# Batch 0's second softmax with the tokens on the partitions: products by chunks of 128 tokens, the way back by TensorE

## The chip, the cores and the metric

The kernel runs on one core of one Trainium2 chip. The metric is the device time of one execution in microseconds (us); smaller is better. Engines are called by the names of the profile: PE (TensorE's matmuls), PEld (its weight loads), DVE (VectorE), ACT (ScalarE), POOL (GpSimd), SP (SyncE, which issues the DMAs here).

## The reference

For each of 8 batches and 8 heads 32 packed rows `p` attend over 576 keys (first softmax), and 576 queries `q` attend over the 32 packed rows (second softmax). The result, read as 4608 tokens by 512, goes through a gated feed-forward layer. All data are fp32.

```python
def sm_attn(qq, kk, vv):
    s = scale * np.matmul(qq, kk.transpose(0, 1, 3, 2))
    s = s - np.max(s, axis=-1, keepdims=True)
    a = np.exp(s)
    a = a / (np.sum(a, axis=-1, keepdims=True) + 1e-09)
    return np.matmul(a, vv)
p_packed = sm_attn(p, k, v)
out = sm_attn(q, p_packed, p_packed)
...
return (x @ w_a) * (x @ w_b) @ w_out
```

## The kernel before

The second attention's value product is folded into the weights: with `pp` the packed rows, `g = pp @ w` for each tile of 128 columns of `w_a` and `w_b` (`g_tiles`, L382), and the layer's first product is then the softmax weights times `g`. The weights of the second softmax, called a2, lie with 4 heads x 32 packed rows on the 128 partitions and the 576 tokens along the row; there are two such groups, e = 0 and 1. a2 and `g` are both split into a high part (`a2_hi`, `ghi`, rounded to the fp32r type) and the rest (`a2_lo`, `glo`), and each product is made of three: hi x hi, hi x lo, lo x hi.

Batch 0 goes first and its chain of steps has nothing to run beside it but the conversion of the weights: load q, k, v, p; turn them by TensorE (`turn_first`, L141, one step `k0`..`k4`, `q0`..`q4` each); first softmax (`stage1`, L265, steps `S0`, `S1`, `r0`, `r1`); `turned` (L254, step `P0`) puts the packed rows into `ppT`; second softmax (`stage2`, L335, steps `s0` for e = 0 and `s1` for e = 1); the first `g` (`next_g`, L594, step `g`); then the loop over 12 column tiles ft (`mm1`, L419), each with two halves of six units, a unit being one pair of `ghi`/`glo` with `a2_hi`/`a2_lo` over 2 x 288 tokens, and then the layer's second product (`mm2_part`). The rest of the kernel (batches 1 to 7) follows without a break.

The second softmax of batch 0, for each e, as the lines stand: L341 makes the scores in PSUM, 8 products with 32 columns of `ppT` as weights and 288 tokens moving, so the packed rows lie on the partitions; L346 (DVE) turns each 32x32 block, which brings the tokens to the partitions in blocks and the 32 scores of one token into a row; L350 (DVE) takes the maximum over these 32; L353 subtracts it (POOL for e = 0, DVE for e = 1); L355 (ACT) is exp; L359 to L361 (DVE) sum and reciprocal; L362 multiplies (POOL for e = 0, DVE for e = 1); L366 (DVE) turns the blocks back; L372 (ACT) writes `a2_hi`; L374 writes `a2_lo` (DVE for e = 0, POOL for e = 1, by way of `lo_part`, L93).

The order of every engine is written out by hand: `START` (L528) is the list of steps up to the first `mm1`, and `PLAN_0` (L539) is what is put between the halves of the loop over ft. Each engine runs its instructions in the order in which these lists emit them. Beside the steps above the lists hold: `A`, `B`, `C`, the three steps that convert one piece of weights (L201 on ACT; L209 on ACT or L206 on DVE or POOL, by the digit of `WAYS`: 0, 1, 2; L212 on DVE), a piece being 128 x 512 words, with four pieces needed for one `g_tiles`; `D`, a split of `w_out`; `L..`, loads; and `X`, `Y`, `Z` with a number, so many products of zeros (L592) that keep TensorE running while it has nothing else. `X` takes a bank of the pool of two single banks, `Z` a pair of banks of the pool of two pairs called m, `Y` the one pair called s. The scores of e = 0 lie in the pair s, those of e = 1 in a pair m. `FIRST` is the order of the first loads, `TURN` picks DVE or ACT for the copies of `turn_first`, `SUBS`, `MULS`, `LOWS`, `HLO`, `WLO` pick the engine of single steps.

## Time and profile before

| what | value |
|---|---|
| median of 3 runs | 708.05 us (707.85 to 708.61) |
| profiled execution, its own time | 707.41 us |
| its span | 705.6 us |
| PE busy | 699.4 us (99%), 5654 matmuls |
| PEld busy | 582.8 us (83%) |
| DVE, ACT, POOL busy | 455.9 us (65%), 356.9 us (51%), 417.1 us (59%) |
| chain that ended last, by engine | PE 91%, DVE 4%, ACT, DMA, SP and issue 1% each |

The page gives the busy time of each engine and the chain of work that ended last, followed back from the end. A matmul's row lasts longer than the time after which the next can start, so a busy PE says little about small gaps: these are read from the starts of neighbouring rows. The first `mm1` starts 31.16 us after the span's start; what comes ahead of it is the stretch that the change rewrites.

### The profile page before, as it was taken

Reading aid. Unit: us, or ns where it says so; the run is one execution under the profiler, and the core shown is the slowest. Engines: PE = TensorE matmul, PEld = TensorE weight load, DVE = VectorE, ACT = ScalarE, POOL = GpSimd, SP = SyncE. Lnnn points to the kernel's source line nnn. Section 1 sums busy time; section 2 is a strip of 40 time slices with the busy share of each in tenths; the row PEclk is TensorE's granted clock in tenths of the full one; section 3 lists DMA queues with packets and bytes.
Section 4 is the critical chain, followed back from the end, with each engine's and each line's share of the span. In section 5 each row is a group of like instructions: output and inputs, shape, how many; then the busy total and the mean of one; then the engine's idle time right before and its main releaser. Section 6 shows DMA issues by size and latency. Waiting matters only on the chain.

```text
span 705.6 us, 14386 instructions
## 1 busy us (share of the span) xinstructions
PE 699.4 (99%) x5654; PEld 582.8 (83%) x5654; DVE 455.9 (65%) x833; ACT 356.9 (51%) x719; POOL 417.1 (59%) x321
## 2 busy tenths in 40 slices
PE   9999999999999999999999999999999999999998
PEld 7888878898788888878888788888888878888886
DVE  4997765467365679566775678765785667754332
ACT  3778724554244555535554455554545446544520
POOL 1596741337254777646863589566775578856520
PEclk9999999999999999999999999999999999999999
DMA  9999986753254736356434664556145323133002
GB/s 316 380 229 297 282 233 136 252 106 93 69 141 161 170 89 172 115 139 168 119 95 124 173 161 95 131 165 173 63 123 154 106 91 119 60 124 117 1 1 75
DMA packets 179460, 102.65 MB, mean 145 GB/s; under 512 B 145728, under 2 KB 161344, under 8 KB 174016
## 3 DMA queue, kind: packets, MB, share of 16 engines
q1 hardware_dynamic: 179392, 101.73, 50.7%
q8 instruction: 44, 0.72, 0.4%
q14 instruction: 24, 0.20, 0.1%
HBM read 85.98 MB, written 15.73 MB: 144 GB/s over the span
## 4 chain that ended last, share of the span: by engine, by line
PE 91%; DVE 4%; issue 1%; DMA 1%; ACT 1%; SPq 1%; DVEq 0%
PE x L754 36%; PE m L796 28%; PE m L414 11%; PE m L440 5%; PE x L810 4%; PE s L326 2%; PE s L341 1%; PE x L396 1%; PE s L280 1%; DMA qn<-in_q_dram 1%; PE s L316 1%; DVE a_lo L93 1%; DVE part L764 0%; DVE d L878 0%; DVE w_ab L212 0%
## 5 line engine op out<-in xcount | busy, mean ns | idle before, releaser
L754 PE MATMUL x<-wo,h_hi 128*128 128x512 f32 (+1 forms) x776 | 249.4, 391 | 0.0
L93 POOL TENSOR_TENSOR h_lo<-asb,h_hi 128x576 fp32r<-128x576 f32 x95 | 139.0, 1465 | 76.0 <-ACT h_hi L841 42.8
L754 PEld LDWEIGHTS x<-wo,h_hi 128*128 128x128 f32 x776 | 140.8, 188 | 22.1 <-ACT part L762 0.8
L754 PE MATMUL x<-wo,h_lo 128*128 128x512 f32 (+1 forms) x388 | 152.2, 392 | 0.0
L93 POOL TENSOR_TENSOR G_lo<-gs,G_hi 128x640 fp32r<-128x640 f32 x72 | 113.1, 1577 | 29.6 <-ACT G_hi L831 29.4
L754 PEld LDWEIGHTS x<-wo,h_lo 128*128 128x128 f32 x388 | 72.9, 188 | 11.7
L93 POOL TENSOR_TENSOR A_lo<-gs,A_hi 128x256 fp32r<-128x256 f32 x36 | 27.2, 755 | 89.3 <-ACT A_hi L819 89.3
L878 DVE TENSOR_TENSOR d<-m,d 128x576 f32<-128x576 f32 (+1 forms) x73 | 54.1, 741 | 34.7 <-ACT d L874 33.9
L891 DVE TENSOR_TENSOR asb<-m,d 128x288 f32<-128x288 f32 x72 | 32.5, 451 | 63.2 <-ACT c L887 59.9
L887 ACT COPY c<-m 128x288 f32<-128x288 f32 x72 | 28.8, 400 | 82.5 <-PE m L796 82.5
L764 DVE TENSOR_TENSOR part<-x,part 128x512 f32<-128x512 f32 (+1 forms) x65 | 44.1, 678 | 38.8 <-PE x L754 38.8
L796 PE MATMUL m<-tx_hi,G_hi 128*128 128x288 f32 x216 | 63.8, 296 | 0.0
L796 PE MATMUL m<-tx_hi,G_lo 128*128 128x288 f32 x216 | 63.6, 295 | 0.0
L796 PE MATMUL m<-tx_lo,G_hi 128*128 128x288 f32 x216 | 63.2, 293 | 0.0
L816 ACT COPY gs<-x 128x512 f32<-128x512 f32 x35 | 20.6, 588 | 82.2 <-PE x L810 80.6
L831 ACT CAST G_hi<-gs 128x640 fp32r<-128x640 f32 x72 | 52.2, 729 | 15.7 <-POOL gs L825 15.1
L874 ACT COPY d<-m 128x576 f32<-128x576 f32 (+1 forms) x73 | 46.7, 640 | 19.2 <-PE m L796 18.8
L841 ACT CAST h_hi<-asb 128x576 fp32r<-128x576 f32 x72 | 49.0, 680 | 11.5 <-DVE asb L905 11.5
L796 PEld LDWEIGHTS m<-a_hi,G_hi 128*128 128x128 f32 x144 | 27.0, 187 | 31.9 <-issue 17.4
L825 POOL TENSOR_TENSOR gs<-gs 128x512 f32<-128x512 f32 x36 | 46.7, 1297 | 3.2 <-DVE gs L822 2.9
L796 PE MATMUL m<-a_hi,G_hi 128*128 128x288 f32 x144 | 46.6, 324 | 0.0
L904 DVE TENSOR_TENSOR m<-m,c 128x288 f32<-128x288 f32 x72 | 33.3, 463 | 17.0 <-PE m L796 15.3
(189 smaller groups left out, 1568.9 us busy)
## 6 DMA issues: line engine op xcount, KB each, us to landing
wr<-w_kept SPq DMA_DIRECT2D x36, 1024.0 KB, 5.1
nat<-in_k_dram SPq DMA_DIRECT2D x56, 144.0 KB, 4.7
nat<-in_q_dram SPq DMA_DIRECT2D x56, 144.0 KB, 5.3
vt<-in_v_dram SPq DMA_DIRECT2D x28, 256.0 KB, 3.9
out_dram<-part SPq DMA_DIRECT2D x27, 256.0 KB, 2.1
raw<-in_moe_w_a_dram SPq DMA_DIRECT2D x12, 512.0 KB, 8.7
raw<-in_moe_w_b_dram SPq DMA_DIRECT2D x12, 512.0 KB, 8.7
raw<-in_moe_w_out_dram SPq DMA_DIRECT2D x12, 512.0 KB, 6.9
```

The costliest lines, as they stand in the source:

```text
L93: return eng.tensor_tensor(out=dst, in0=src, in1=hi.bitcast(F32), op=ALU.subtract)
L414: nc.tensor.matmul(out=ps[:, half, 0:HS], lhsT=gt[:, kt, ft % 4, cols], rhs=at[:, kt, HS * half:HS * half + HS], start=(n == 0 and kt == 0 ...
L440: nc.tensor.matmul(out=o[:, cols], lhsT=ht[:, c0:c0 + P], rhs=wt[:, cols], start=(ft == 0 and n == 0), stop=(ft == NFT - 1 and n == 2))
L754: nc.tensor.matmul(out=o[:, cols], lhsT=ht[:, c0:c0 + P], rhs=wt[:, cols], start=(ft == fts[0] and n == 0), stop=end)
L764: nc.vector.tensor_tensor(out=parts[i][:, cols], in0=o[:, cols], in1=parts[i][:, cols], op=ALU.add)
L796: nc.tensor.matmul(out=bank[:, n % 2, 0:HS], lhsT=g, rhs=t, start=(first and i == 0), stop=(i == 2), skip_group_check=True)
L825: nc.gpsimd.tensor_tensor(out=gs[:, 2:4].rearrange("p a u f -> p a (u f)"), in0=gs[:, 0:2].rearrange("p a u f -> p a (u f)"), in1=s2.unsqu ...
L831: nc.scalar.copy(out=G_hi[:, n % 3], in_=gs[:, 1:6, n % 2])
L841: nc.scalar.copy(out=view(h_hi[ft]), in_=src)
L874: nc.scalar.copy(out=d[:, both], in_=X[:, both, 0:HS])
L878: nc.vector.tensor_tensor(out=d[:, both], in0=V[:, both, 0:HS], in1=d[:, both], op=ALU.add)
L904: nc.vector.tensor_tensor(out=v, in0=v, in1=c2, op=ALU.add)
```

## The change

For batch 0 alone `stage2` makes the scores with the tokens on the partitions. For each e there are 24 products in place of 8: for chunks c = 0 and 1 the weights are 128 tokens of `q` (64 rows x 128 columns) and the 32 columns of `ppT` move; for c = 2 the weights are the last 32 tokens. L346's turn goes; the maximum reads PSUM; the difference reads PSUM and is on DVE for both e. Exp, sum, reciprocal and product stay. L366's turn back goes: for each e TensorE turns four blocks of 128 x 128 and makes eight products of 32 x 32 with the identity, into a pair of banks; `a2_hi` (ACT) and `a2_lo` (DVE for both e) read that pair. The first `g`'s two low parts become steps of their own. The first `mm1` runs its twelve units in the order of `MIX` (ten units, the copy of the first half, two units). `START`, `PLAN_0`, `FIRST` and the strings of engines are new: the zero products between the second softmax's scores and `g` are 25 in place of 50, `k0 p0 k1 q0 v0 v1 q1` is the order of the first loads, and the same conversions lie at other places. `PLAN_0` is cut here to its first line.

```diff
@@ -336,21 +336,34 @@
 
         TU = 2 * XH
         x = bank_pair(b > 0 or e == 0)
-        for r in range(R):
-            for u in range(2):
-                nc.tensor.matmul(
-                    out=x[J * r:J * r + J, u, 0:HS], lhsT=ppT[64 * u:64 * u + 64, 1 if u ^ e else 2 * (b % 2), r, :],
-                    rhs=xT_cols(b, "q", u, 2 * r + e), start=True, stop=True)
+        qk = lambda u, r: ppT[64 * u:64 * u + 64, 1 if u ^ e else 2 * (b % 2), r, :]
+        for c, r, u in [(c, r, u) for c in (range(3) if b == 0 else (0,)) for r in range(R) for u in range(2)]:
+            xT = xT_cols(b, "q", u, 2 * r + e)
+            if b:
+                nc.tensor.matmul(out=x[J * r:J * r + J, u, 0:HS], lhsT=qk(u, r), rhs=xT, start=True, stop=True)
+            elif c < 2:
+                at = P * c + J * r
+                nc.tensor.matmul(out=x[:, u, at:at + J], lhsT=xT[:, P * c:P * c + P], rhs=qk(u, r), start=True, stop=True)
+            else:
+                nc.tensor.matmul(out=x[J * r:J * r + J, u, 2 * P:HS], lhsT=xT[:, 2 * P:HS], rhs=qk(u, r), start=True, stop=True)
         yield
         s2 = work(b, f"s2_{e}", [P, TU, J], "t1")
-        nc.vector.transpose(out=s2.rearrange("p (u x) j -> p u (x j)", u=2), in_=x[:, :, 0:HS])
+        if b:
+            nc.vector.transpose(out=s2.rearrange("p (u x) j -> p u (x j)", u=2), in_=x[:, :, 0:HS])
         if b > NB:
             yield
         mx = sm.tile([P, TU], F32, name="mx")
-        nc.vector.tensor_reduce(out=mx, in_=s2, axis=AX, op=ALU.max)
+        four = lambda t: t.rearrange("p (u x) j -> p u x j", u=2)
+        raw2 = s2 if b else x[:, :, 0:HS].rearrange("p u (x j) -> p u x j", j=J)
+        nc.vector.tensor_reduce(
+            out=mx if b else mx.rearrange("p (u x) -> p u x", u=2), in_=raw2, axis=AX, op=ALU.max)
         yield
         on = lambda flags: nc.vector if b < 2 and flags[2 * b + e] == "1" else nc.gpsimd
-        on(SUBS).tensor_tensor(out=s2, in0=s2, in1=mx.unsqueeze(2).broadcast_to([P, TU, J]), op=ALU.subtract)
+        peak = mx.unsqueeze(2).broadcast_to([P, TU, J])
+        if b:
+            on(SUBS).tensor_tensor(out=s2, in0=s2, in1=peak, op=ALU.subtract)
+        else:
+            nc.vector.tensor_tensor(out=four(s2), in0=raw2, in1=four(peak), op=ALU.subtract)
         yield
         nc.scalar.activation(out=s2, in_=s2, func=AF.Exp, scale=scale)
         yield
@@ -361,6 +374,22 @@
         nc.vector.reciprocal(out=sum2, in_=sum2)
         on(MULS).tensor_tensor(out=s2, in0=s2, in1=sum2.unsqueeze(2).broadcast_to([P, TU, J]), op=ALU.mult)
         yield
+        if b == 0:
+            y = bank_pair(e == 1)
+            for u in range(2):
+                at = s2[:, XH * u:XH * u + XH, :].rearrange("p x j -> p (x j)")
+                for c in range(2):
+                    nc.tensor.transpose(y[:, u, P * c:P * c + P], at[:, P * c:P * c + P], ident)
+                for r in range(R):
+                    z = slice(J * r, J * r + J)
+                    nc.tensor.matmul(out=y[z, u, 2 * P:HS], lhsT=at[z, 2 * P:HS], rhs=ident[z, z], start=True, stop=True)
+            a2f = y[:, :, 0:HS].rearrange("p u (x l) -> p u x l", l=TL)
+            hi, lo = (t[:, e, :].rearrange("p (x u l) -> p u x l", u=2, l=TL) for t in (a2_hi, a2_lo))
+            nc.scalar.copy(out=hi, in_=a2f)
+            yield
+            lo_part(lo, a2f, hi)
+            yield
+            return
         halves = b >= NB
         a2f = work(b, f"a2f_{e}", [P, 2, XH, TL], "t1" if halves and e else "t2")
         nc.vector.transpose(out=a2f.rearrange("p u x l -> p (u x l)"), in_=s2.rearrange("p x j -> p (x j)"))
@@ -397,10 +426,15 @@
                         out=gps[e][J * r:J * r + J, 0:2 * P * n], lhsT=ppT[rows, 2 * (b % 2), r, :],
                         rhs=w if n == 2 else w[:, fts[0] % 2], start=True, stop=True)
             parts = [(x, slice(0, E))] if x is not None else [(gps[e][:, 0:2 * P * n], e) for e in range(E)]
+            lows = []
             for part, e in parts:
                 hi, lo = (t[:, e, i] if n == 1 else t[:, e, i:i + 2].rearrange("p u c -> p (u c)") for t in (ghi, glo))
                 nc.scalar.copy(out=hi, in_=part)
-                lo_part(lo, part, hi)
+                if s and b == 0:
+                    lows.append((lo, part, hi))
+                else:
+                    lo_part(lo, part, hi)
+        return lows
 
 
     def mm1_half(i, ft, ps=None, kts=range(E)):
@@ -416,16 +450,33 @@
                     start=(n == 0 and kt == 0), stop=(n == len(steps) - 1 and kt == E - 1))
         return ps
 
+    def first_units(ps, order, n0, n1):
+
+        halves = [i for i, _ in order]
+        for n in range(n0, n1):
+            i, unit = order[n]
+            kt, what = divmod(unit, 3)
+            gt, at = ((ghi, a2_hi), (ghi, a2_lo), (glo, a2_hi))[what]
+            for half in range(2):
+                nc.tensor.matmul(
+                    out=ps[i][:, half, 0:HS], lhsT=gt[:, kt, 0, P * i:P * i + P], rhs=at[:, kt, HS * half:HS * half + HS],
+                    start=i not in halves[:n], stop=i not in halves[n + 1:])
+
     def mm1(b, ft, between):
         asb = sm.tile([P, 2, HS], F32, name="asb")
         if b == 0 and ft == 0:
-            pa, pb = (mm1_half(i, ft, kts=(0,)) for i in range(2))
-            mm1_half(0, ft, pa, (1,))
+            order = [divmod(int(x, 16), 6) for x in MIX]
+            last = max(n for n, (i, _) in enumerate(order) if i == 0)
+            pa, pb = both = bank_pair(), bank_pair()
+            first_units(both, order, 0, last + 1)
+            nc.scalar.copy(out=asb, in_=pa[:, :, 0:HS])
+            between()
+            first_units(both, order, last + 1, 12)
         else:
-            pa, pb = mm1_half(0, ft), None
-        nc.scalar.copy(out=asb, in_=pa[:, :, 0:HS])
-        between()
-        pb = mm1_half(1, ft, pb, (1,) if pb is not None else range(E))
+            pa = mm1_half(0, ft)
+            nc.scalar.copy(out=asb, in_=pa[:, :, 0:HS])
+            between()
+            pb = mm1_half(1, ft)
         nc.vector.tensor_tensor(out=asb, in0=pb[:, :, 0:HS], in1=asb, op=ALU.mult)
         c0 = 64 * (b % 2)
         hh = h_hi[ft][:, c0:c0 + S]
@@ -524,23 +575,24 @@
 
     st = {}
 
-    FIRST = ("k0 k1 p0 q0 v0 q1 v1 w1 w1 w1 w1 w1 w1 w1 w1 w1 w1 w1")
-    START = ("Y7 k1 X4 k0 T0 k2 k3 k4 q1 B S0 r0 r1 S1 q0 r1 r0 q2 r0 r1 q4 r0 r1 q3 A P0 A X3 Lp2 A s0 s1 s0 "
-             "s1 C Z8 s1 X3 s0 B A B Z9 C B X7 A B C C X5 X15 C s0 A s1 B s0 s1 A B Lk2 B B A s0 B s1 s1 C s0 "
-             "s1 g A")
-    WAYS = ("200000020222122211202100021202110111")
-    TURN = ("1000100010")
-    SUBS, MULS, LOWS = "0101", "0100", "01"
-    HLO, WLO = "000000001000", "000011000011"
+    FIRST = ("k0 p0 k1 q0 v0 v1 q1 w1 w1 w1 w1 w1 w1 w1 w1 w1 w1 w1")
+    START = ("Y8 k1 k0 k2 T0 k3 k4 q1 S0 r0 r1 S1 q0 B r1 r0 r0 r1 r0 q2 A r1 q3 q4 P0 A s1 Lp2 s0 s1 A C s0 B "
+             "C B C X8 s1 s0 B A B C A Y12 A C Z1 s0 X2 B B s0 B s1 Z2 Lk2 B A s0 A s1 B s1 s0 s1 s1 C A g g g "
+             "A")
+    WAYS = ("220000010222122211100100021212120112")
+    TURN = ("0010100010")
+    SUBS, MULS, LOWS = "1010", "0111", "01"
+    HLO, WLO = "000000001101", "000011000011"
+    MIX = "019428a7356b"
 
     PLAN = (" |  |  | S0 | r0 | r0 |  | r0 |  | r0 Lv1 ; S1 | r1 | r1 q0 Lk2 | r1 | r1 | q1 Lk3 Lv2 P0 |  ; s0 | s0 s0 | s0 T2 | "
             "s0 Lp4 | s0 s1 | s1 s1 | s1 | s1 | s1 | t0 t1 t2 t3 u0 | k2 |  | k3 Lq2")
     PLAN = dict(enumerate(PLAN.split("|")))
-    PLAN_0 = ("Lk1 A A B C B C B A C | C B C | A A B | B C A A C A C | | B Lp2 C Lv0 B | | | C k0 T0 B | A A C "
...
+    PLAN_0 = ("A B C B Lk1 A C B C B C | B C | A A A A | B C A Lp2 B C | C | B A C | | | C k0 T0 A A B | C Lv0 "
...
     PLAN_0 = dict(enumerate(PLAN_0.split("|")))
 
     pieces = [(c, n) for c in range(NC) for n in range(4)] + [(NC, f) for f in range(NFT)]
@@ -593,7 +645,9 @@
 
     def next_g(b):
 
-        g_tiles(b, *(((0, 1), (2,)) if b else ((0, 1),)), s=True)
+        for lo, part, hi in g_tiles(b, *(((0, 1), (2,)) if b else ((0, 1),)), s=True):
+            yield
+            lo_part(lo, part, hi)
         yield
 
     ET = mybir.EngineType
```

## Rows read from the trace of the kernel before

**Rows 1.** The table of windows, two of its stretches: start and end, length, then for PE, PEld, DVE, ACT, POOL the busy time with the number of instructions, PE's granted clock, the DMA engines' share, GB/s.

```profile
35.00:45.00 10.00, 10.00 (x91) 8.16 (x76) 8.56 (x12) 8.70 (x17) 9.51 (x7) 1.00 0.92 202
225.00:706.00 481.00, 477.12 (x3590) 396.78 (x3588) 308.96 (x583) 235.69 (x488) 308.32 (x241) 1.00 0.42 117
```

**Rows 2.** The chain of work that ended last, pieces between 17 and 35 us: start, length, engine, tile and line.

```profile
17.26 0.73 PE s L341 x16
...
18.01 0.79 DVE s L346
...
22.24 2.49 DVE w_ab L212 x4
...
27.58 0.99 DVE s L362
28.57 0.70 DVE a2f L366
...
29.29 1.33 ACT a_hi L372 x2
30.62 0.49 ACT ghi L402
...
31.16 3.72 PE m L414 x24
```

**Rows 3.** The same chain between 71 and 78 us.

```profile
71.42 0.59 ACT ghi L402
72.01 0.55 ACT asb L426
...
72.60 5.07 PE m L414 x36
```

**Rows 4.** The timeline of SP's queue: start, length, line and what is loaded (the second part of q, then the second group of v).

```profile
5.15 0.45 SPq L138 DMA_DIRECT2D qn<-in_q_dram  x1
...
6.15 0.39 SPq L170 DMA_DIRECT2D vt<-in_v_dram  x1
```

**Rows 5.** The DMA view of the same two loads: size and us from issue to landing.

```profile
qn<-in_q_dram SPq DMA_DIRECT2D x1, 640.0 KB, 6.4
...
vt<-in_v_dram SPq DMA_DIRECT2D x1, 512.0 KB, 7.2
```

**Rows 6.** The timeline of PE: start, length to the last end, line, tiles, rows x columns of the weights, what moves, and how many instructions (an fp32 product is two).

```profile
1.05 3.36 PE L592 MATMUL s<-zero 128*128 128x128 f32 x14 [1.05 <-DVE zero L77]
...
12.19 0.66 PE L316 MATMUL x<-ident,a 128*128 128x128 f32 x4
...
13.64 0.38 PE L152 MATMUL x<-ident,qn 128*128 128x128 f32 x2
13.95 1.78 PE L326 MATMUL x<-vt,a1T 128*32 128x64 f32 x80
...
17.19 0.72 PE L341 MATMUL s<-qT,ppT 64*32 64x288 f32 x16
17.70 0.70 PE L341 MATMUL m<-qT,ppT 64*32 64x288 f32 x16
...
20.88 2.17 PE L592 MATMUL m<-zero 128*128 128x128 f32 x18
...
29.02 1.21 PE L396 MATMUL x<-w_ab,ppT 64*32 64x512 f32 x16
31.16 0.54 PE L414 MATMUL m<-a_hi,ghi 128*128 128x288 f32 x2 [0.93 <-ACT ghi L402]
```

**Rows 7.** Single lines' instructions between 14 and 45 us (L592, L341) and 31 and 35 us (L414): shortest, median and longest duration in ns, first and last start, form.

```profile
L592 PE MATMUL m<-zero x34: 275/275/377, 18.3 to 22.8; 128*128 128x128 f32 x34
...
L341 PE MATMUL s<-qT,ppT x16: 402/413/427, 17.2 to 17.5; 64*32 64x288 f32 x16
...
L414 PE MATMUL m<-a_hi,ghi x8: 294/297/402, 31.2 to 34.1; 128*128 128x288 f32 x8
```

**Rows 8.** The timeline of PEld, the weight loads of L341's first group.

```profile
17.19 0.19 PEld L341 LDWEIGHTS s<-qT,ppT 64*32 64x32 f32 x16
```

**Rows 9.** The timeline of DVE between 20 and 30 us.

```profile
20.30 0.76 DVE L350 TENSOR_REDUCE mx<-s 128x18 f32<-128x576 f32 x1
20.97 0.69 DVE L212 SCALAR_TENSOR_TENSOR w_ab<-raw 128x512 uint32<-128x512 uint32 x1
21.57 0.75 DVE L353 TENSOR_TENSOR s<-s,mx 128x576 f32<-128x576 f32 x1
...
24.65 0.75 DVE L359 TENSOR_REDUCE sum<-s 128x18 f32<-128x576 f32 x1
25.43 0.18 DVE L360 TENSOR_SCALAR sum<-sum 128x18 f32<-128x18 f32 x1
25.64 0.27 DVE L361 RECIPROCAL sum<-sum 128x18 f32<-128x18 f32 x1
...
28.49 1.42 DVE L366 STREAM_TRANSPOSE a2f<-s 128x576 f32<-128x576 f32 x2
```

**Rows 10.** The timeline of POOL, one line.

```profile
26.06 1.16 POOL L362 TENSOR_TENSOR s<-s,sum 128x576 f32<-128x576 f32 x1 [5.23 <-DVE sum L361]
```

**Rows 11.** The timeline of ACT, two lines.

```profile
22.81 0.66 ACT L355 ACTIVATE s<-s 128x576 f32<-128x576 f32 x1
...
24.52 0.67 ACT L209 ACTIVATE raw<-raw 128x512 uint32<-128x512 uint32 x1
```

8 rows, old and new, of the table PLAN_0 are left out of this document.

## The prediction

> **What bounds the kernel now.** I read the table of windows first. From 35 us on PE is busy through, at a granted clock of 1.00 [rows 1]; the chain of work that ended last is PE's own from 31.16 us on, but for one short detour [rows 2, 3]. There the pair of banks is free only when ACT's copy ends, and L414 goes on at 72.60 in place of 72.35 (the last unit's end by its spacing): 0.25 us [rows 3]. So from 31.16 us on the time is the sum of PE's products, the change alters none of them after that point, and what it is worth is how far the first unit of mm1 moves, plus waits of PE that it makes or takes away later. The first unit waits 0.93 us for ACT's ghi [rows 6]. Followed back, the chain ahead of it is: scores on PE at 17.2 (17.26 in the chain, since the first row's weight load is not in it), DVE from 18.01 to 29.27 nearly without a break (turns, maxima, differences, five conversions C, sums, product, turn back), then ACT's two a2_hi and ghi [rows 2]. DVE is the bound of this stretch, and conversions of weights lie inside its chain: four of them take 2.49 us, 0.60 us each by their spacing [rows 2].
>
> **The first loads and turns.** The second part of q was issued at 5.15 and landed 6.4 us later, at 11.55; v's second group landed at 13.35 [rows 4, 5]. They change places, so q lands near 13.35. In the new list its turn q2 comes behind the first half of the packed rows' product, which by the first softmax's rows isn't done before 14.1, so the delay is hidden by that chain, with 0.7 us to spare. k's turns come some 0.4 us earlier (no X4 ahead of them), and then q2, q3, q4 lie in PE's and DVE's queues close ahead of P0, where before q2 and q4 lay in waits: I take 0.4 us earlier and 0.4 us later as one sum, nothing, and leave 0.4 us on both sides. The scores start at 17.2 as before.
>
> **The new scores.** This is the term that decides, and no row shows such a product (128 columns of weights, 32 moving). What the rows show: the first product of zeros after a pause lasted 377 ns where the others lasted 275, and the first L414 402 where the shortest lasted 294 [rows 7]; so a load of 128 fp32 columns that nothing hides takes 0.10 to 0.11 us. L341, with 32 columns, has 427 against 402, 0.025 us, a fourth. In the stream of zeros the spacing is (2.17 - 0.28)/17 = 0.111 us with a load in each [rows 6]: there 128 columns move for 0.107 us and hide the load. With 32 columns moving only some 0.03 us can hide it, and the load itself sets the pace. Sixteen loads of L341's eight places (two row groups times four column groups) are all done in 0.19 us though each lasts 0.10 [rows 8], so loads into different places run side by side; I take it that the two row groups u = 0 and 1 do so here too. For each e chunks 0 and 1 are 2 x 4 x 2 products = 32 instructions, 16 in each row group: 16 x 0.11 = 1.76 us. The 16 small instructions of chunk 2 and two changes of shape add 0.25 (the change from L152 to L326 leaves 13.95 - 13.64 - 2 x 0.11 = 0.09 us [rows 6]). So 2.0 us for each e, 4.0 in all, against 0.51 each before (17.19 to 17.70 [rows 6]). Lower bound: 48 instructions at the spacing of the narrow L326, 1.71/80 = 0.021 [rows 6], is 1.0 us; upper bound: the row groups one after another, 32 x 0.11 + 0.25 = 3.8 us. I take 2.0, since the 0.11 is the very load that is made here, only with 64 rows.
>
> The Trainium skill, page "TensorE: Matmul & The Clock Gate", section "Part 3: Packing small matmuls — row/col tiling", says that a weight load overlaps a matmul in flight only where the row group differs. By it a place pays load and move, 0.134 us, and e takes 16 x 0.134 + 0.25 = 2.4 us. The stream of zeros speaks against it: all its products use the same rows, and 0.111 us between starts leaves no room for a load of 0.10 behind a move of 0.107 [rows 6, 7].
>
> **DVE after the scores.** Order in the new list: maximum e1, C, maximum e0, C, C, difference e1, difference e0, C, C, sum e0. The scores of e1 end at 19.2 and cover maximum e1 and one C; those of e0 end at 21.2, and DVE sees them 0.3 us later, as with L341 (17.70 to 18.01), at 21.5. Then maximum 0.68, two C 1.2, difference e1 0.68 and e0 0.75 (L353's row [rows 9]; PSUM as the source I price like SBUF): 24.8. Exp e0 takes 0.66 [rows 11] under cover of two C (to 26.0); without them the sum would start at 25.5. Sum, eps, reciprocal: 25.64 + 0.27 - 24.65 = 1.26 us [rows 9], to 27.2. The product of e0 on POOL takes 1.16 [rows 10], to 28.4. One B, then e1's sum to 28.8 and its product of 0.9 to 1.0 us [rows 2], to 29.75. Removed are four turns of 0.7 to 0.8 us [rows 2, 9], 2.9 us of DVE; put back are e0's difference (0.75) and, later, a2_lo of e1 (0.75).
>
> **The way back.** Y12 needs the pair s, so it waits for the difference of e0 (24.85); Y12, Z1, X2, Z2 are 34 instructions of 0.111 us [rows 6], to 28.65, 0.2 later than the product of e0. The way back of one e: four turns of 0.11 (128 columns move, as with the zeros; L316's four fit in 0.66 with their first load and tail [rows 6]) = 0.44, 16 small instructions in four places 0.1, four changes of shape 0.36: 0.9 us, between 0.55 (no changes) and 1.4 (the small ones at 0.05 each). So e0 is back at 29.55, e1 from 29.8 to 30.7, and only then come g's products on PE, 1.15 us (L396's 1.21 with its tail [rows 6]), to 31.85. ACT meanwhile: a2_hi of e0, A, a2_hi of e1 from 30.95 to 31.6, A 0.57 (as L209 [rows 11]) to 32.2, ghi 0.58 (0.53 by spacing): 32.8. The first unit starts at 32.85: 1.7 us later than before. Before, g's products lay in the shadow of the turns on DVE; now they stand behind TensorE's own turns.
>
> **The first mm1 and the rest.** Before, its 24 instructions took 3.72 us [rows 2], 0.3 more than at the spacing of the next groups, mostly waiting for glo. MIX puts glo's first use at the fifth unit, so up to 0.3 us comes back; I count 0.1, because glo0 and C stand behind a2_lo of e1 on DVE. The moved conversions, HLO, MULS and SUBS cost nothing while PE is full: DVE had 1.4 and ACT 1.3 us idle in 10 just after the start, POOL 0.5 [rows 1]. If that cover is gone, PE waits at a g or a pair of banks as at 72.35, 0.3 to 1 us a time. The 0.25 us there may go or stay; I leave it. The pair that mm1's second half writes is freed by a2_lo of e0, done by 31.6: no wait.
>
> **Sum.** +1.7 - 0.1 = +1.6 us: span 705.6 to 707.2, the profiled execution's own time 707.41 to 709.0. The median is 0.64 above that execution, so 708.05 + 1.6 = 709.65, given as 709.7. Of one us more in the scores of each e the end gets two; with the term at 1.8 to 2.3 us and T0 and the way back off by a few tenths the forecast case spans 708.9 to 711. Within 0.2% (1.4 us, about what a measurement of this kernel can tell from no change) lies what stays under 709.5.
>
> **The rivals.**
> 1. Scores at 1.0 us for each e or less, because loads of four column groups at a time are as quick as L341's [rows 8]. Then e0's scores end at 19.2 and DVE, not PE, is the bound: from 18.5 two maxima, three C, two differences, 4.6 us, to 23.1; everything behind is 1.7 us earlier, mm1 starts at 31.15, and mm1's 0.3 us comes back: 707.8, not slower. It decides from below 1.2 us a group. For it: the loads of L341 do run side by side. Against it: there each load is a fourth as long.
> 2. The same with scores of 0.5 us, the first turns' 0.4 us earlier kept, and both PE waits (0.3 and 0.25) gone: 22.6 for the differences, mm1 at 30.25 and 1.4 us in all: 706.6, faster. Only if every price falls to its floor.
> 3. The two row groups load one after another: 3.8 us each, 1.8 x 2 more: 713.3.
> 4. By the rule of the page named above, with its load behind the move: 2.4 us each, 0.8 more: 710.5.
> 5. PE's clock. Between X8's end (23.0) and Y12 PE now has nothing for 1.9 us; before, the zeros filled that stretch. At the start of the span the same zeros came over 0.2 us apart, at half the rate (14 in 3.36 with the last one's tail [rows 6]). If the clock falls to 1.2 GHz there, 34 zeros and the way back take twice as long, up to 4 us; a fall for part of it, or new waits in the loop, some 2.5: 712.2.
>
> **How the numbers follow.** Forecast case 0.49 (0.30 of it beyond 709.5, 0.19 within), rival 1 0.22, rival 2 0.05, rival 3 0.10, rival 4 0.06, rival 5 0.08. Slower: 0.30 + 0.10 + 0.06 + 0.08 = 0.54; same: 0.19 + 0.22 = 0.41; faster: 0.05. The range leaves out rival 2, rival 3 and the edge of rival 1: 707.5 to 712.6. The forecast case alone: 708.9 to 711.0.
>
> **What would show it.** In the new profile: the span of L341's successor, 24 products for each e, near 2.0 us with starts of one row group 0.11 apart (the main step); DVE waiting for PE at the first maximum and again at the second; the maximum of e0 near 21.5 and the difference of e0 ending near 24.8; PE empty for about 2 us ahead of Y12; the first L414 near 32.9, waiting for ghi behind an A; then PE full. The prediction is wrong if the scores of a group take 1.2 us or less, if the first unit starts ahead of 31.5, or if PE waits in the loop for more than 0.5 us in all.

## The result, and the profile after

| | median us | runs | mean granted clock | ratio to before, 95% |
|---|---|---|---|---|
| before | 707.95 | 707.15 to 709.44 (6) | 1.00 | |
| after | 714.35 | 712.48 to 717.39 (6) | .990 to .998 | 1.0091 [1.0076, 1.0107] |

Slower by 6.4 us, where 1.6 were forecast, and outside the range. The profiled execution of after took 712.48 us with a span of 710.7, 5.1 more than before. It is also the quickest of the six runs and the one with the highest clock, so a part of the loss shows only in the other runs.

The timeline of PE in the kernel after shows the start (start, length to the last end, line, tiles, rows x columns of the weights, what moves, instructions; in brackets the idle time ahead and who ended it):

```profile
7.97 0.66 PE L152 MATMUL m<-ident,kn 128*128 128x128 f32 x4 [1.76 <-DMA kn<-in_k_dram]
...
18.68 1.98 PE L346 MATMUL m<-ppT,qT 64*128 64x32 f32 x32 [0.75 <-DVE ppT L261]
20.58 0.29 PE L348 MATMUL m<-ppT,qT 64*32 64x32 f32 x16
20.80 1.98 PE L346 MATMUL s<-ppT,qT 64*128 64x32 f32 x32
...
23.00 3.56 PE L644 MATMUL x<-zero 128*128 128x128 f32 x16
26.59 2.92 PE L644 MATMUL s<-zero 128*128 128x128 f32 x24
...
30.46 0.38 PE L382 MATMUL m<-ident,s 128*128 128x128 f32 x2
...
31.53 0.44 PE L382 MATMUL s<-ident,s 128*128 128x128 f32 x2
...
32.65 1.09 PE L425 MATMUL x<-w_ab,ppT 64*32 64x512 f32 x16
34.53 0.53 PE L461 MATMUL m<-a_hi,ghi 128*128 128x288 f32 x2 [0.79 <-ACT ghi L432]
```

Read against [rows 6] these lines split the start. The scores begin at 18.68 instead of 17.19, 1.49 later, and the first row says why: k's third turn stood 1.76 us for the second part of k. From the scores' start to the first mm1 it is 15.85 us instead of 13.97, 1.88 more; 1.7 was forecast. So the first mm1 comes 3.37 us later.

The timeline of DVE in the kernel after answers to [rows 9]:

```profile
23.16 0.76 DVE L358 TENSOR_REDUCE mx<-s 128x18 f32<-128x576 f32 x1 [0.81 <-PE s L348]
...
25.70 0.75 DVE L366 TENSOR_TENSOR s<-s,mx 128x576 f32<-128x576 f32 x1
```

Counted from the scores' start, the maximum of e0 begins 4.48 us behind it (forecast 21.5 - 17.2 = 4.3) and the difference of e0 ends 7.77 behind it (forecast 7.6).

The table of windows of the kernel after (length, then PE, PEld, DVE, ACT, POOL with instructions, granted clock, DMA share, GB/s):

```profile
22.00:23.00 1.00, 1.00 (x31) 0.90 (x29) 0.34 (x1) 0.90 (x3) 0.00 (x0) 0.88 1.06 383
23.00:24.00 1.00, 1.00 (x15) 1.00 (x5) 0.84 (x2) 1.00 (x2) 0.00 (x0) 0.50 1.04 383
...
26.00:27.00 1.00, 0.96 (x7) 0.80 (x7) 1.00 (x3) 0.52 (x1) 0.00 (x0) 0.91 1.06 389
```

The number behind POOL's bracket, the granted clock, is new: from 22.8 to 26.2 us the granted clock is 0.50, the lower of TensorE's two levels (1.2 GHz of 2.4). In the trace of the kernel before it does not fall until the last matmul is done. PE was busy all through the four microseconds ahead of the fall. In this run the fall cost the chain little, since X8's zeros lay there (16 in 3.56 us) and PE would have stood for DVE's differences anyway. The five runs without a trace had lower mean clocks, .990 to .995, so there the lower level lasted longer.

The rest is in the loop: 672.47 us from the first mm1 to the start of the last matmul, 670.82 before, 1.65 more. The view of waits of PE from 36 to 700 us in the kernel after (who waited, for whom, us in total, times, longest):

```profile
PE m L448 <- ACT asb L477: 0.7, 1, 0.7
PE s L326 <- ACT t L298: 0.6, 1, 0.6
PE m L850 <- DVE a_lo L93: 0.3, 1, 0.3
```

The same view of before names no wait. The prediction had set more than 0.5 us of such waits as a sign of being wrong; here they are 1.6. The sum of the profiled run: 1.49 + 1.88 + 1.65 = 5.0 of the 5.1 us. Not all of the 1.65 can be put down to the change: the last of the three waits, 0.44 us by the starts, stands in the trace of every other run below, those with the loop of before included (e6_narrow_zeros, e7_before_loads, e13_delay10, e14_delay19: 671.2 to 671.4 us), and is missing only in the one trace of before.

### The profile page after: what moved, and what is told of

Read it like the earlier page. It is cut to its first block, busy times and chain, and to the rows that moved or that the text cites. A ratio compares the mean times of both kernels' runs of the same rounds, so it can differ in the third digit from the quotient of the medians.

```text
span 710.7 us, 14475 instructions
## 1 busy us (share of the span) xinstructions
PE 700.1 (99%) x5702; PEld 582.8 (82%) x5702; DVE 458.3 (64%) x836; ACT 356.5 (50%) x718; POOL 410.0 (58%) x315
## 4 chain that ended last, share of the span: by engine, by line
PE 90%; DVE 4%; DMA 2%; ACT 2%; issue 1%; SPq 0%; DVEq 0%; ACTq 0%
PE x L808 36%; PE m L850 27%; PE m L448 8%; PE m L491 5%; PE x L864 4%; PE s L326 2%; PE s L343 1%; PE s L280 1%; DVE a_lo L93 1%; DMA raw<-in_moe_w_out_dram 1%; PE x L425 1%; PE s L316 1%; DMA kn<-in_k_dram 1%; PE x L644 1%; DVE part L818 1%
## 5 line engine op out<-in xcount | busy, mean ns | idle before, releaser
L93 POOL TENSOR_TENSOR h_lo<-asb,h_hi 128x576 fp32r<-128x576 f32 x93 | 136.1, 1465 | 84.2 <-ACT h_hi L895 43.1
L958 DVE TENSOR_TENSOR m<-m,c 128x288 f32<-128x288 f32 x72 | 33.3, 463 | 16.9 <-PE m L850 15.2
```

Source lines behind the costliest of these rows:

```text
L93: return eng.tensor_tensor(out=dst, in0=src, in1=hi.bitcast(F32), op=ALU.subtract)
L958: nc.vector.tensor_tensor(out=v, in0=v, in1=c2, op=ALU.add)
```

## The experiments

All columns are from results and traces; "mm1" is the start of the first mm1, "loop" the time from there to the start of the last matmul of the same profiled run. Each kernel was measured beside before, whose medians were 707.95 to 708.62, so kernels are compared by their ratios. Waits in the loop are counted from the starts of neighbouring matmuls, less their usual spacing; the brackets in the rows, counted from the end of a row, are some 0.17 us shorter.

| run | median us | ratio, 95% | mm1 | loop |
|---|---|---|---|---|
| before | 707.95 | | 31.16 | 670.82 |
| after | 714.35 | 1.0091 [1.0076, 1.0107] | 34.53 | 672.47 |
| e1_first | 712.38 | 1.0057 [1.0045, 1.0070] | 34.85 | 672.15 |
| e2_zeros | 715.74 | 1.0108 [1.0091, 1.0125] | 38.74 | 671.61 |
| e3_both | 715.31 | 1.0097 [1.0083, 1.0110] | 39.04 | 671.66 |
| e4_twice | 719.13 | 1.0146 [1.0131, 1.0162] | 40.27 | 671.67 |
| e5_wide | 711.58 | 1.0042 [1.0030, 1.0054] | 33.28 | 673.41 |
| e6_narrow_zeros | 709.47 | 1.0017 [1.0007, 1.0027] | 32.54 | 671.21 |
| e7_before_loads | 713.11 | 1.0068 [1.0056, 1.0080] | 35.95 | 671.35 |
| e8_before_plan | 709.53 | 1.0016 [1.0008, 1.0025] | 31.06 | 672.79 |
| e9_wide_oldplan | 711.74 | 1.0046 [1.0034, 1.0059] | 33.04 | 673.82 |
| e10_wide_alone | 713.59 | 1.0066 [1.0053, 1.0079] | 36.08 | 671.52 |
| e11_wide_twice | 712.01 | 1.0047 [1.0034, 1.0060] | 35.34 | 671.35 |
| e12_piece_later | 711.97 | 1.0055 [1.0042, 1.0069] | 33.07 | 673.23 |
| e13_delay10 | 709.99 | 1.0024 [1.0014, 1.0034] | 33.17 | 671.30 |
| e14_delay19 | 712.50 | 1.0057 [1.0044, 1.0069] | 34.97 | 671.26 |
| e15_k_later | 713.61 | 1.0076 [1.0063, 1.0088] | 32.94 | 675.24 |
| e16_hlo | 711.82 | 1.0041 [1.0028, 1.0053] | 33.07 | 673.62 |
| e17_oldplan_matched | 710.27 | 1.0023 [1.0014, 1.0032] | 32.99 | 671.64 |

### Loads, and the first theory of the clock

**e1_first**: the changed kernel with the old order of the first loads.

```
-    FIRST = ("k0 p0 k1 q0 v0 v1 q1 ...
+    FIRST = ("k0 k1 p0 q0 v0 q1 v1 ...
```

> The changed kernel with the old order of the first loads (k, k, p, q, v, q, v). Theory: of the 6.4 us lost some 1.5 lie in the load of k's second part, which landed at 7.9 us in the changed kernel against 6.2 before; so k's second turn starts near 6.3 us, the new scores near 17.2 to 17.5 in place of 18.7, and the first unit of mm1 near 33.2 in place of 34.5. What the clock takes varies from run to run and stays, unless the shorter pause ahead of k's turn is its cause. Median 711.5 to 713. Rival, the order of the loads is hidden by the first softmax: scores still at 18.5 or later, median 714.

The scores began at 17.25, so the 1.49 us are of the load order; the median fell by 2.0, as expected. But the first mm1 did not come earlier (34.85 for 34.53), and the profiled runs took the same time, 712.47 and 712.48: the gain of the median lies against the runs of after that have no trace. The timeline of PE in e1_first:

```profile
17.25 1.98 PE L346 MATMUL m<-ppT,qT 64*128 64x32 f32 x32 [0.76 <-DVE ppT L261]
...
19.44 3.62 PE L346 MATMUL s<-ppT,qT 64*128 64x32 f32 x32
```

The same 32 instructions took 1.98 us for e1 and 3.62 for e0: the clock fell at 19.2, in the middle of the scores, and stayed at the lower level to 26.0. In the profiled run the clock took what the loads gave.

**e2_zeros** and **e3_both** fill PE's pauses of the start with zeros, e3_both with the old loads too:

```
-    START = ("Y8 k1 k0 k2 T0 ... S1 q0 B r1 ... P0 A s1 Lp2 ... C B C X8 s1
+    START = ("Y8 k1 k0 X8 k2 T0 ... S1 q0 Z4 B r1 ... P0 X3 A s1 Lp2 ... C B C X15 s1
```

> The changed kernel with more zero products where PE was empty ahead of the second softmax and behind its scores (X8 ahead of k2, Z4 behind q0, X3 ahead of the scores, X15 in place of X8). Theory: the granted clock falls to 1.2 GHz because PE has pauses and narrow products one after another from 12 to 23 us; with the pauses filled it stays at 2.4 in all or nearly all runs (mean clock 0.999 or more), the spread of the runs shrinks to 2 us, and the median falls by 1.5 to 3 us, to 711.5 to 713. Rival A, the narrow products alone make it fall: the clock still falls near 22 us, runs still at 0.990 to 0.998, median 714. Rival B, the clock falls but hits only zeros, so it costs nothing: clock restored, median unchanged.

> Both: the old order of the first loads and the zeros. Theory: what is left over the kernel before is the new scores and the way back, 1.7 to 2 us at the first unit of mm1 (near 33.1), and the wait of 0.7 to 1.0 us in batch 1 that the changed kernel's profile showed behind the stores, if that belongs to the plan: median 709.7 to 711. Rival, the loss lies in the loop and batch 1: median over 712.5.

Both missed; in the clock e2_zeros' rival A held. With PE's pauses filled the clock still fell, at 22.6 us in either, to 29.4, and the zeros put the scores at 20.0 and 20.3. So the pauses, my theory until then and the mechanism of rival 5, are not what brought the clock down here. **e4_twice** is e3_both with the second chunk's products made twice, to price the scores:

```
-        for c, r, u in [... for c in (range(3) if b == 0 ...
+        for c, r, u in [... for c in ((0, 1, 1, 2) if b == 0 ...
```

> As e3_both, with the products of chunk 1 made twice (32 in place of 24 for each group; same output). Theory: each group's scores take 2.12 + 0.95 = 3.05 us, and the end follows with twice the difference: 1.9 us over e3_both, first unit of mm1 1.9 later. Rival, another chain (POOL's conversions, loads of weights) bounds the first unit and the scores have room: less than 1 us over e3_both.

It cost 3.8 us of the median and 1.23 us at the first mm1, for 1.9 expected; the clock fell within the doubled scores, so the price is mixed with it, and e11_wide_twice does it cleanly.

### Where the clock fell, and where it stayed

**e5_wide** is e1_first with 128 columns moving instead of 32; **e6_narrow_zeros** does the reverse in the kernel before, with products that nobody reads.

```
e5:  -  nc.tensor.matmul(out=x[:, u, at:at + J], lhsT=xT[:, P * c:P * c + P], rhs=qk(u, r), ...)
     +  nc.tensor.matmul(out=x[:, u, at:at + P].rearrange("p (n j) -> p n j", j=J),
     +      lhsT=xT[:, P * c:P * c + P], rhs=qk(u, r).unsqueeze(1).broadcast_to([64, P // J, J]), ...)
e6:  -  nc.tensor.matmul(out=x, lhsT=zero, rhs=zero, ...)
     +  cols = J if 14 <= woken[0] < 34 else P
     +  nc.tensor.matmul(out=x[:, 0:cols], lhsT=zero, rhs=zero[:, 0:cols], ...)
```

> The changed kernel with the first loads in the old order (as e1_first), and the 16 products of each e that moved 32 columns now move 128: the same 32 columns four times over. The surplus columns fall on places that a later product overwrites, so the scores stay what they were. The products of the changed kernel started 0.11 us apart in each row group however few columns they moved, so the path should not notice: scores still about 2.1 us per e at full clock. Theory A (products that move few columns make the granted clock fall): the clock stays at its upper level from 6 us to the end, mean clock 1.00; scores at 17.25, their last instruction near 21.4, first mm1 near 33.1 (e1_first: 34.85), median 709.5 to 711. Theory B (the clock falls for another reason, the idle stretches around the scores or the turn back, say): the clock falls again somewhere from 19 to 27 us, mean clock .994, median 712 to 713 as e1_first. Theory C (128 columns do cost time): last score instruction after 23, first mm1 later than 34.85.

> The kernel before, with one edit: the 20 products of zeros behind its scores (18.3 to about 22.9 us) move 32 columns instead of 128. Nothing reads them, and each took 0.11 us a pass, the time that the changed kernel's narrow products took too, so the chain of the softmax is untouched. Theory A (few moving columns bring the clock down): the clock of the kernel before, at its upper level from 6.13 us on in every run, falls to its lower level between 20 and 25 us, for 3 to 7 us; the zeros behind take twice as long, g starts 1 to 3 us later than 29.02, median 709 to 711.5. Theory B (the clock's fall in the changed kernel has to do with idle stretches or with the chain): nothing falls, PE stays as busy as it was, median 707.8 to 708.3.

Theory A held in both, in the clock, the scores, the first mm1 and g; only e5_wide's median is 0.6 above what I expected, for the loop's sake (below). The timeline of PE in e5_wide and two lines of its table of windows:

```profile
17.31 2.06 PE L346 MATMUL m<-ppT,qT 64*128 64x128 f32 x32 [0.75 <-DVE ppT L261]
...
19.52 2.06 PE L346 MATMUL s<-ppT,qT 64*128 64x128 f32 x32
...
25.34 2.92 PE L646 MATMUL s<-zero 128*128 128x128 f32 x24 [1.56 <-DVE s L368]
```

```profile
22.00:23.00 1.00, 1.00 (x11) 1.00 (x11) 1.00 (x2) 0.83 (x2) 0.00 (x0) 1.00 1.03 379
...
24.00:25.00 1.00, 0.00 (x0) 0.00 (x0) 1.00 (x2) 0.07 (x1) 0.00 (x0) 1.00 1.05 387
```

Four times the columns take 2.06 us in place of 1.98, while the 16 instructions with 32 columns of weights take 0.2 (20.58 to 20.80 in after): at this size the time goes with the weights that are loaded, not with what moves. The mean clock was .999 to 1.000 in all five runs, and in the trace it stayed at its upper level, with PE standing for 1.56 us behind the scores, the very pause from which rival 5 feared the fall. In e6_narrow_zeros the timeline of PE and then the table of windows read:

```profile
20.77 2.17 PE L595 MATMUL m<-zero 128*128 128x32 f32 x18
22.79 7.90 PE L595 MATMUL x<-zero 128*128 128x128 f32 x54
```

```profile
23.00:24.00 1.00, 1.00 (x6) 1.00 (x6) 1.00 (x2) 1.00 (x3) 0.00 (x0) 0.50 1.05 387
```

The narrow zeros last to the hundredth what the wide ones of before last (2.17 for 18 [rows 6]), PE's busy share is 1.00 either way, and yet the clock falls behind them and g starts at 30.62 instead of 29.02. In ten of its twelve runs the mean clock was .994 to .998 and the time 709.16 to 711.22; in the other two it was 1.000 and the time 708.01 and 708.36.

**e10_wide_alone**: the wide products with the changed order of loads (e5_wide without its edit of FIRST).

> The changed kernel with one edit: its 16 products of each e move 128 columns instead of 32 (the same 32 four times over), everything else as changed, the order of the first loads too. Theory (the granted clock's fall is of the narrow products and costs 2 us and more of the median): clock 1.00 in every run, scores at 18.7, median 711.6 to 712.6 instead of 714.35, and the runs within 1.3 us of each other instead of 4.9. Rival (the fall cost little, since the profiled run of the changed kernel had it between 22.8 and 26.2 us while TensorE only waited, and the runs differ for another reason): median 713.8 to 714.8.

The median came between the two expectations, 0.8 us below after's and 1.8 by the ratios, and the clock was 1.00 in one run of five (711.96). In the profiled one of the other four it fell earlier. The timeline of PE in e10_wide_alone, then one line of its table of windows:

```profile
8.10 0.72 PE L152 MATMUL m<-ident,kn 128*128 128x128 f32 x4 [2.15 <-DMA kn<-in_k_dram]
```

```profile
9.00:10.00 1.00, 1.00 (x7) 1.00 (x6) 0.43 (x1) 0.53 (x1) 0.00 (x0) 0.50 1.10 288
```

PE stands for k's second part for 2.15 us, and the clock falls at 8.6, behind that. So in this run the load order cost twice, the wait and the clock behind it. In the trace of after, behind 1.76 us of the same wait, the clock did not fall. **e7_before_loads**, the kernel before with the changed FIRST alone, shows the same at another place.

> The kernel before, with the changed kernel's order of the first loads alone (p between k's halves, v's second half ahead of q's). Theory A (k's second half comes later and the turns wait for it, which sets the scores): k's third turn near 8.0 instead of 7.29, scores near 18.5 instead of 17.19, first mm1 near 32.5 instead of 31.16, median 709.0 to 709.6. Rival: the first softmax has slack enough that the order is hidden in the kernel before, as my prediction had it: median 707.7 to 708.2.

It is 4.7 us slower than before, some four times what I expected, mostly because the old START turns q's second part ahead of the first softmax's turns. The timeline of PE in e7_before_loads:

```profile
15.33 1.11 PE L152 MATMUL m<-ident,qn 128*128 128x128 f32 x4 [2.94 <-DMA qn<-in_q_dram]
```

Behind that wait the clock falls, at 15.2, and the first softmax's turns run at the lower level. So this run does not price the load order alone; e1_first against after does, with what the clock did in either.

### The scores at full clock, and the way through the loop

**e11_wide_twice**: e5_wide with the edit of e4_twice.

> e5_wide with the second chunk's products made twice, the same result written twice over: 8 products more for each e, at full clock this time. The 16 of an e took 2.0 us, so 1.0 us more for each e, 2.0 in all. Theory (the scores stand on the path at their full length, as my prediction priced them): first mm1 at 35.0 to 35.4 instead of 33.28; of that the loop gives back up to 1.0, since entered late it doesn't wait for its weights, so median 712.3 to 713.6. Rival (VectorE's pieces between the maxima and the differences fill the time): first mm1 below 34.0, median within 0.4 of e5_wide.

The first mm1 moved by 2.06 us for 2 x 1.0 us more on PE: the scores lie on the path at full length. But the median rose by 0.4, since the loop took back all of it, 671.35 instead of 673.41, where I had allowed up to 1.0. Entered at 33.3, the loop with the new lists loses 2 us; entered at 35.3 it doesn't. **e8_before_plan** puts the new loop lists (PLAN_0, the loop's part of WAYS, HLO, WLO, batch 1's SUBS and MULS) into the kernel before:

```
-    SUBS, MULS, LOWS = "0101", "0100", "01"
-    HLO, WLO = "000000001000", "000011000011"
-    PLAN_0 = ("Lk1 A A B C B C B A C | ...
+    SUBS, MULS, LOWS = "0110", "0111", "01"
+    HLO, WLO = "000000001101", "000011000011"
+    PLAN_0 = ("A A B C B Lk1 A C B C B C | ...
```

> The kernel before, with the changed kernel's lists for the loop alone: which preparations stand between the products from 31 us on, and which engine does the low words, batch 1's differences and its multiplications; first loads, start and scores are as they were. Theory (the 1.7 us that the changed kernel lost between 84 us and the end come from the new lists): median 709.0 to 709.8, with the loss between 120 us and 620 us. Rival (they come from the phase in which the loop is entered, or from the transfers of that one run): median 707.7 to 708.4.

1.1 us slower, and the loop 1.97 longer than in the one trace of before, with nothing else changed. The view of waits of PE in e8_before_plan names three, the last of them the one that every trace but before's has:

```profile
PE s L326 <- ACT t L298: 0.6, 1, 0.6
PE m L414 <- ACT asb L426: 0.5, 1, 0.5
PE m L796 <- DVE a_lo L93: 0.3, 1, 0.3
```

The chain of waits in e8_before_plan around the first of them:

```profile
75.18 1.04 DVE h_lo L93
76.22 0.34 DVE raw L206
76.56 0.60 DVE wo_f L212
77.16 0.68 DVE nmx L286
...
78.05 0.84 ACT t L298 x2
...
78.93 0.90 PE s L326 x40
```

Batch 1's maximum (nmx) stands in DVE's line behind a low word and two pieces, and its exponential's reader is PE. **e16_hlo** gave that low word back to POOL in e5_wide:

```
-    HLO, WLO = "000000001101", "000011000011"
+    HLO, WLO = "000000001000", "000011000011"
```

> e5_wide with one list entry as before: the low words of h are made on GpSimd again for the two tiles (9 and 11) that the change gave to VectorE. In e5_wide the path at 76.9 to 80.7 us went through VectorE's line: low word of h 1.05, two pieces, then batch 1's maximum, the exponential behind it, and TensorE stood 0.75 us at 79.8. Theory (that wait is of the new engine list): no wait above 0.3 at 78 to 81, first mm2 near 82.9 instead of 83.66, median 710.6 to 711.2 (e5_wide: 711.58). Rival (the low word on GpSimd ends later and its reader waits instead): first mm2 at 83.5 or later, median 711.3 to 712.

The rival held: the wait grew (PE stood 1.31 us at 79.1). The timeline of POOL in e16_hlo, then that of DVE:

```profile
75.36 1.30 POOL L93 TENSOR_TENSOR wo<-wo_f,wo 128x512 fp32r<-128x512 f32 x1 [1.51 <-ACT wo L237]
76.62 1.62 POOL L93 TENSOR_TENSOR h_lo<-asb,h_hi 128x576 fp32r<-128x576 f32 x1
```

```profile
75.41 1.53 DVE L206 TENSOR_SCALAR raw<-raw 128x512 uint32<-128x512 uint32 x1
76.86 1.92 DVE L212 SCALAR_TENSOR_TENSOR wo_f<-raw 128x512 uint32<-128x512 uint32 x1
78.71 0.74 DVE L286 TENSOR_REDUCE nmx<-s 128x1 f32<-128x576 f32 x1
```

The two pieces on DVE, 0.42 and 0.68 us in e5_wide at this place, ran beside POOL's low words and took 1.53 and 1.92, so that the maximum started hardly earlier (78.71 for 78.81). A word given to POOL can be paid for on DVE when the two overlap. The same shows at the wait that only before's trace lacks. The timelines of DVE and POOL in after, then in before:

```profile
610.08 1.88 DVE L93 TENSOR_TENSOR a_lo<-t,a_hi 128x288 fp32r<-128x288 f32 x1
610.10 1.55 POOL L93 TENSOR_TENSOR G_lo<-gs,G_hi 128x640 fp32r<-128x640 f32 x1
```

```profile
605.79 0.45 DVE L93 TENSOR_TENSOR a_lo<-t,a_hi 128x288 fp32r<-128x288 f32 x1
605.81 1.85 POOL L93 TENSOR_TENSOR G_lo<-gs,G_hi 128x640 fp32r<-128x640 f32 x1
```

The two begin 0.02 us apart in both, and once DVE's word takes four times as long, once POOL's is longer by 0.3; PE waits 0.44 us for a_lo where DVE's is the long one.

**e9_wide_oldplan** is e5_wide with the old loop lists (e8's diff reversed).

> e5_wide with the lists for the loop of the kernel before (preparations between the products from the first mm1 on, engines of the low words, of batch 1's differences and multiplications); the start, the softmax and the first products are as in e5_wide. Theory (the new lists cost some 1.1 us of the median, as e8_before_plan gave): first mm1 at 33.3 as in e5_wide, first mm1 to first mm2 in 49.4 instead of 50.38, median 710.1 to 710.8. What is left over the kernel before is then the softmax's longer chain, 2.1 us at the first mm1. Rival (the loop loses as much with any lists when it is entered at 33.3, for weights that land by a pace of their own): median 711.3 to 712.

Nothing gained, which looked like the rival. But the kernel mixed two lists that don't match: the changed START does one high word more than the old one, so the old list ran one tile ahead of the weights. The chain of waits in e9_wide_oldplan:

```profile
40.63 4.81 DMA raw<-in_moe_w_a_dram
...
45.53 0.04 ACT raw L201
...
46.09 0.63 ACT asb L479
...
46.77 3.33 PE m L450 x23
```

ACT stands in order for a weight tile that isn't there, the copy asb waits behind it, and PE for asb, 1.79 us. Two runs are edits of this kernel, waits and all: **e12_piece_later** moves one piece of START, **e15_k_later** one transfer of PLAN_0:

```
e12: -  ... s1 s1 C A g g g A")       e15: -  PLAN_0 = ("Lk1 A A B C B C B A C | C B C | A A B | ...
     +  ... s1 s1 C g g g A A")            +  PLAN_0 = ("A A B C B C B A C | C B C | Lk1 A A B | ...
```

> e9_wide_oldplan with one preparation piece on ScalarE (a high word of a weight tile, 0.7 us) moved from ahead of g's copies to behind them: in e5_wide it ran from 32.07 to 32.75, and the first high word of g behind it began at 32.65, with the first mm1 waiting for that. Theory (a piece in ScalarE's line costs the first mm1 what it takes there, less the time that g's products still need): first mm1 at 32.7 to 32.9 instead of 33.3, median 0.3 to 0.6 below e9_wide_oldplan. Rival (g's products end at 32.5 to 32.7 anyway and set it, or the loop waits for the piece instead): median the same within 0.2.

> e9_wide_oldplan with the eight loads of batch 1's k put two products' stretches later, behind the weight loads that stand there. In e9_wide_oldplan the loop stood 1.79 us at 44.5 us for a weight tile whose load was issued at 40.63, behind four of those k loads, and landed at 45.45. Theory (that order costs the wait): the load is issued before 37, no wait above 0.5 us at 44 to 47, first mm2 near 81.9 instead of 83.51, median 709.8 to 710.8. Rival (the wait comes back elsewhere, for k itself or for the next weights): first mm2 after 83, median 711.3 to 712.

In e12_piece_later the rival held: the first mm1 at 33.07 instead of 33.04, since g's own products end as late. e15_k_later missed its target: the four loads of k ahead of the late tile are those of START's Lk2, and Lk1 stands behind it. The wait came at 44.5 us as in e9_wide_oldplan, 1.93 us for 1.79, and the loop took 1.4 us more. In the profiled run that is the clock's: it fell behind this wait, from 47.2 to 50.6 us, and the products that start at 46.8 in both kernels are 1.55 us apart five microseconds later. One run with a mean clock of 1.000 took 713.12, however, so the clock does not account for all five. The run tells nothing for either theory.

**e13_delay10** and **e14_delay19** add zeros ahead of g to the kernel before and nothing else:

```
-  ... C s0 s1 g A")
+  ... C s0 s1 Z10 g A")      (Z19 in e14_delay19)
```

> The kernel before with ten products of zeros (2.2 us) ahead of g, nothing else: the first mm1 moves from 31.16 to about 33.3, where e5_wide and e9_wide_oldplan enter the loop. Theory A (entered there, the loop meets its transfers and stores badly, whoever enters it): first mm1 to last matmul 672.8 to 673.8 us instead of 670.8, last matmul near 706.5, median 711 to 712.3. Theory B (what the changed start does besides, its pieces and their places, costs the loop 2.6 us): first mm1 to last matmul stays at 670.8 to 671.4, last matmul near 704.3, median 709.8 to 710.6. Theory C (the kernel before has slack): median within 0.5 of before.

> The same with nineteen products of zeros (4.2 us): the first mm1 near 35.3, where e11_wide_twice entered. Theory A: the loop is done from there in 671.4 as in e11_wide_twice, so that the last matmul comes at 706.7, no later than with ten: median 711.3 to 712.3. Theory B: 2 us more than with ten: last matmul 706.3, median 711.8 to 712.6, and ten are at 710.2. The two differ here only together with e13_delay10: A has the two within 0.6 of each other, B 2 us apart.

Theory B: the old loop takes 671.3 us from either entry, and the delays of 2.0 and 3.8 us at the first mm1 come out as 2.5 and 4.25 at the last matmul, each with the same 0.44 us at 609 to 611, the wait for DVE's a_lo. So the entry's time alone is not what costs e5_wide its 2 us; the new lists cost them at that entry, and at a later one (e11_wide_twice) they don't. **e17_oldplan_matched** mends e9_wide_oldplan:

```
-    PLAN_0 = ("Lk1 A A B C B C B A C | ...
+    PLAN_0 = ("Lk1 A B C B C B A C | ...
```

> e9_wide_oldplan with the first high word of the old loop list left out, since the changed start has done it already; nothing is left out of the computation. Theory (the loop's 2 us are of its lists): the wait of 1.79 us at 44.5 us goes, first mm1 at 33.1 and from there 671.2 to 671.8 us to the last matmul as in e13_delay10, median 709.8 to 710.6. Rival (they are of the places of the start's pieces): first mm1 to last matmul 672.5 or more, median 711 or more.

It came out as the theory had it, in all its numbers: mm1 at 32.99, the loop 671.64, the median 710.27. Its PE starts as e5_wide's does; the timeline of PE in e17_oldplan_matched:

```profile
17.01 2.06 PE L346 MATMUL m<-ppT,qT 64*128 64x128 f32 x32 [0.75 <-DVE ppT L261]
...
32.99 0.54 PE L463 MATMUL m<-a_hi,ghi 128*128 128x288 f32 x2 [0.79 <-ACT ghi L434]
```

No version beat the kernel before.

## Why the prediction was wrong

By the ratios (times 708 us) the 6.4 us of after come down in three steps, each one edit apart: old loads 2.4 (after to e1_first), wide products 1.1 (to e5_wide), old loop lists 1.3 (to e17_oldplan_matched). Left is 1.0023 [1.0014, 1.0032], 1.6 us: the new softmax with its START. The steps are no prices by themselves, since the loop with the new lists answers to its entry: the wide products bring the first mm1 1.57 us forward (34.85 to 33.28), and the loop takes 1.26 of it back (672.15 to 673.41). The prediction's sum was +1.6. What it worked out was right within some tenths; that the sum agrees to the tenth is luck, since the two traces are 2.65 us apart at the last matmul, 1.83 of it at the first mm1. What it set to nothing was not nothing.

**The scores (right).** 1.98 us for the 32 instructions and 0.2 behind them, 2.12 for each e by the starts (18.68, 20.80); forecast 2.0. The rivals of 1.0 and 3.8 us are out. e5_wide bears out the reason, a pace set by the load, and e11_wide_twice the place on the path: 2.06 us for 2.0. Rival 4, from the Trainium skill, page "TensorE: Matmul & The Clock Gate", section "Part 3: Packing small matmuls — row/col tiling", is out as well: with its load behind the move, four times the columns would lengthen each of the 16 products of a row group by the longer move, and e5_wide took 2.06 us in place of 1.98. That section names the background weight buffer as a second case in which a load runs ahead, which the prediction left out. The 0.107 us of a move, from which that rival was priced, stands in no row by itself: the zeros' 0.111 holds load and move together [rows 6].

**DVE and the way back (right, a little short).** DVE's steps up to the sum of e0 came within 0.2 us of the forecast, counted from the scores. The way back took 1.07 and 1.12 us (30.46, 31.53, 32.65), forecast 0.9, in its bounds. The first mm1 waits 0.79 us for ghi behind an A, as said. 1.88 us in all for the 1.7 forecast. The first mm1's 24 instructions take 3.39 us to the next products (34.53 to 37.92) instead of 3.66, so MIX gave back 0.27 of its 0.3, for the 0.1 counted.

**The first loads ("I take 0.4 us earlier and 0.4 us later as one sum, nothing"; wrong, 2.4 us with the clock).** This is the step that failed first. I followed q and v, which change places. But FIRST also puts p's two loads ahead of k's second part. The timeline of SP in the kernel before, then in the kernel after:

```profile
0.74 0.86 SPq L138 DMA_DIRECT2D kn<-in_k_dram  x2
```

```profile
0.73 0.38 SPq L138 DMA_DIRECT2D kn<-in_k_dram  x1
1.16 1.33 SPq L188 DMA_DIRECT2D p_nat<-in_p_dram  x2
2.54 0.60 SPq L138 DMA_DIRECT2D kn<-in_k_dram  x1
...
7.94 0.35 SPq L138 DMA_DIRECT2D qn<-in_q_dram  x1
```

Both parts of k were issued by 1.6 us; now the second is at 2.54. With the 5.4 us from issue to landing that the DMA view of after has for it, it lands at 7.94, and the turn starts at 7.97. In before that turn started at 7.29 and in e1_first at 6.28, without a wait; nothing covers the delay. That q's delay was covered is luck: its second part was issued at 7.94, not at 6.15, and with the 7.0 us to landing of the DMA view it came at 14.94, not at 13.35. In after its turn starts at 15.42, late by k; in e1_first, with k in time, it starts at 13.98, so by these numbers PE would have waited for q if k had been in time.

**The clock (rival 5, 0.08; the size and the cause wrong).** I priced a fall from a pause ahead of Y12. That pause came (1.56 us in e5_wide) and did no harm. The clock fell where I had counted full work: at the narrow products. They cost 1.1 us by e1_first against e5_wide, and 1.4 us at the first mm1 where e6_narrow_zeros puts them into the kernel before. In the runs of after it varies most: a mean clock of .990 is 0.010 x 710 x 2 = 14 us at the lower level, and that is the run of 717.39; the profiled one, at .998, has 3.4. Where it fell in the runs without a trace is not shown.

**"The moved conversions, HLO, MULS and SUBS cost nothing while PE is full" (wrong, 1.3 us).** I gave the price of a wait, 0.3 to 1 us a time, and left it out of the sum, by DVE's and ACT's idle shares [rows 1]. The shares were true. The waits that were traced back are of order, not of load: a maximum or a copy for which PE waits stands in line behind a piece. e8_before_plan, which changes the lists alone, and e17_oldplan_matched, which undoes them alone, give 1.1 and 1.3 us at their entries, 31.1 and 33.0 to 33.3.

**Open.** Which entries of the loop lists cost it (e16_hlo took out one and only moved the wait). Why PE waits 0.9 us for ACT's asb at 131 to 134 us in after, e5_wide and e17_oldplan_matched alike, and not in e13_delay10. How the 2.4 us of the loads split into k's wait and the clock: only one run of after has a trace. Why the one trace of before lacks the wait for a_lo.

## What to carry to other kernels

When a list of first loads changes, write down the landing of every load behind each moved one, not only of the two that change places; the first engine that waits sets all the rest. Products whose time is their weight load had TensorE busy at 1.00 here while its granted clock fell: where few columns move for each load, read the granted clock of that stretch and the one behind it, and try more columns, which cost 0.08 us for 32 instructions here. And the idle share of an in-order engine does not price a piece put into its line: look at what stands behind that piece and who waits for it.
